# Attention and channel MLP in one stream: the last down weights, the first stores, the row copies and the start of the projection moved

## The chip, the core and the metric

The kernel runs on one core of a Trainium2 chip. The core has five engines with an instruction queue each: TensorE (PE; matmuls, with weight loads shown apart as PEld), VectorE (DVE), ScalarE (ACT), GpSimd (POOL) and SyncE (SP), which here only issues DMAs. An engine takes its instructions in the order in which the program writes them, so an instruction that waits holds everything behind it on that engine. DMAs are issued from an engine's queue and run beside the engines; instructions wait for their landing. Matmuls read the core's on-chip memory and write banks of PSUM, of which the kernel keeps small pools.

The metric is the device time of one execution in microseconds. Several runs are made and their median is taken.

## What is computed

The input `x` has 2048 tokens of 576 numbers. The result mixes two branches by a gate of each token:

```python
g = sigmoid((x * gate_w).sum(-1, keepdims=True))
a = softmax(q k^T * 18**-0.5) v  @ wo      # 32 heads of 18, q, k, v = x @ wqkv
b = gelu(layernorm(x) @ w1 + b1) @ w2 + b2 # 576 -> 4608 -> 576, tanh form of gelu
out = g * a + (1 - g) * b
```

All of it is float32 in and out. The kernel multiplies in a faster, rounded form of float32: most operands are split into a rounded high part and a low part (what the rounding left over), and a product is the sum of three matmuls (high by high, low by high, high by low).

## The kernel before

**First stage (up to about 255 us).** `x` is loaded in four blocks of 512 tokens, transposed, split and multiplied by `wqkv`. The parts of q and k go to a DRAM buffer `qk_scr`, v to `v_scr` (one store of a token tile behind each second `v_group`, L788), the normalised tokens of the MLP to `y_scr`. In the last block the generator of the MLP is started between the groups; its third step, called as `between()` inside the last `v_group`, loads the low parts of the first y block (`load_y(0, 1, ...)`, six DMAs).

**The loop (512 steps).** Sixteen pairs of heads times two halves of the queries make 32 units `u` of 16 steps `kc`. A step has two half steps. Each computes two banks of scores (`s2`, L247), takes their exponentials on ScalarE (L250) and does a round of the row maxima for the next unit (`s1_round`: matmul L206, maximum on VectorE L208). Every second step multiplies two blocks of probabilities by v (`pv`, L265). When a unit's maxima are all there, `s1_finish` turns them into two rows (high and low part) per head and `rows()` transposes them (L223), copies them to the tile `mr` (L225) and writes them with four DMAs (through `dma_r`, L121) into rows 54, 55, 118 and 119 of the unit's query tile `QA[u % 3]`, so that the score matmul subtracts the maximum by itself. In the loop this happens at step 12 of the unit before. At a unit's end `o_store` copies the sums out (L277) and sends them to DRAM (L279, L285); 12 slots later `spread` takes the reciprocals of the denominators on VectorE (L288) and stores them (L289), and 16 slots after that `wide` writes them out for every row (L297).

**Slots.** `run_due` counts slots: one behind every `s2`, every `pv` and every fill, seven in two steps. `defer(n, fn)` writes `fn` into the program n slots later. `bg` is a list of work for GpSimd, written out when the kernel's own estimate of GpSimd's queue (`pool_end - now`) is below a bound: 950 ns for an up block, 3800 ns for a down block, and its raw data counts as landed (`LOADED`; in the loop 8 slots after the load for an up block). This is all decided when the program is written out, not on the chip.

**The MLP inside the loop.** Three times in two steps `fill` writes a piece of the MLP between the attention's matmuls (`atom`). The MLP has four blocks of 512 tokens (`tb`, their y tiles loaded by `load_y`, L121 `big<-y_scr`) and nine groups `g` in each, 36 groups `i`, two pairs `q` of 128-wide chunks in a group. `h_pair` does the up matmuls of a pair (L443); the gelu of it runs on VectorE, ScalarE (L464, L496, L494) and mostly GpSimd (L162), which ends with a high and a low part `hh`, `hl` of each chunk. `outs` does the down matmuls of a group in four output pairs, one for each tile of 128 tokens (`out_pair`, L523, summed on VectorE L532). In the last group of a block the second pair is put inside `outs` of the group before, ahead of its output pair `t == 2` (`inner`): its `hh` and `hl` are kept in a tile of the up weights' pool.

In the first block the weights are raw: `load_w1` (L346) and `load_w2` (L352) load them into one `x` tile, `split` rounds the high part on ScalarE (L367), takes the low part on GpSimd (L162), and stores both to `w1_scr` and `w2_scr` (L372). In the other blocks they are reloaded from there (L121 `w<-w_scr`). Up weights have three places (`wp1`), down weights four (`wp2`), which is one group: `prep_w2(i)` loads the four tiles of group i once `outs(i - 1)` has been written, and each load waits until its place is read for the last time. When a block is done, its result is scaled by the gate on GpSimd (L536) and stored to `b_scr` (L539).

**The projection.** At steps 489, 494, 497 and 499 (`PSTEP`) the generator `out_proj` is called: it loads `wo` (L890, split on GpSimd L883 and L884), the first block of attention sums (`load_o`), their reciprocals (`load_den`), and plans their product (`normed`: L957 and L967 on VectorE, L960 on ScalarE). Once the MLP is over, its last store has been written (`kept == NT`) and step 500 is past, `fill` writes pieces of the projection (L1030): 14 matmuls for half a row tile, then L1034 on VectorE adds `b` from the tile that `load_b` loaded (L945). What is left follows the loop.

## Time and profile before

| | us |
|---|---|
| median of 3 runs | 2382.97 |
| lowest, highest run | 2378.87, 2385.91 |
| the profiled execution | 2379.91 |
| its span, first to last instruction | 2378.1 |

| engine | busy us | share of the span |
|---|---|---|
| TensorE | 2308.8 | 97% |
| VectorE | 1655.4 | 70% |
| ScalarE | 1425.9 | 60% |
| GpSimd | 968.3 | 41% |

Times within the trace count from the span's start. A row of the timeline gives start, length, engine, line, operation, what it writes and reads (by the program's own names, `out<-in`), the number of instructions merged into it, and in brackets how long the engine had been idle before it and what ended that. "SPq" is SyncE's queue: the length of such a row is the time for which it was issuing, not that of the transfer. The granted clock is the share of TensorE's full clock that it was given in a stretch.

### The profile page before, as it was taken

What the parts mean: (1) busy time and instruction counts of PE and PEld (TensorE: products, weight loads), DVE (VectorE), ACT (ScalarE), POOL (GpSimd) and SP (SyncE); (2) the same over time, 40 slices, a digit from 0 to 9 for tenths busy, and PEclk for the clock granted to TensorE, in tenths of its full rate; (3) what the DMA queues carried; (4) which work ended last, traced back from release to release, by engine and by line L of the source; (5) the groups of instructions that cost most, each with busy time, mean ns of one, the idle gap of its engine ahead of it and who ended that gap; (6) DMA issues with size and microseconds to landing.
All of it is one profiled execution on the core that took longest, in us unless ns stands there. A gap on an engine that the chain in (4) does not pass through costs nothing.

```text
span 2378.1 us, 51603 instructions
## 1 busy us (share of the span) xinstructions
PE 2308.8 (97%) x20585; PEld 1571.9 (66%) x20585; DVE 1655.4 (70%) x2890; ACT 1425.9 (60%) x2628; POOL 968.3 (41%) x964
## 2 busy tenths in 40 slices
PE   8999899999999999999999999999999999999889
PEld 7876566666666666666666666666656666666558
DVE  5467577777776777777777777777767777777424
ACT  4222367777676666666666666666656666666552
POOL 3001366666664433333454444433343334444500
PEclk9999899999999999999999999999999999999899
DMA  7748744545455423342354424232545343331254
GB/s 229 243 166 235 211 146 137 166 129 151 134 185 163 156 94 116 104 140 97 98 153 161 130 85 131 94 116 94 142 137 166 112 119 114 92 115 66 96 181 157
DMA packets 164874, 330.31 MB, mean 139 GB/s; under 512 B 57898, under 2 KB 84558, under 8 KB 153906
## 3 DMA queue, kind: packets, MB, share of 16 engines
q1 hardware_dynamic: 163050, 323.78, 43.4%
q8 instruction: 162, 2.65, 0.5%
q10 hardware_dynamic: 1584, 3.24, 0.4%
q14 instruction: 78, 0.64, 0.1%
HBM read 234.16 MB, written 96.58 MB: 139 GB/s over the span
## 4 chain that ended last, share of the span: by engine, by line
PE 89%; DMA 5%; DVE 3%; SPq 1%; issue 1%; ACT 0%; POOL 0%; DVEq 0%; ACTq 0%
PE ps L523 20%; PE ps L265 19%; PE ps L443 18%; PE ps L247 12%; PE ps L206 11%; PE ps L755 4%; PE ps L1030 2%; PE ps L776 2%; DVE m L208 1%; DMA big<-y_scr 1%; DMA x<-in_B_w_dram 1%; DMA v_scr<-vt 0%; PE ps L682 0%; SPq L121 0%; SPq L372 0%
## 5 line engine op out<-in xcount | busy, mean ns | idle before, releaser
L208 DVE TENSOR_REDUCE m<-ps 128x1 f32<-128x512 f32 x2048 | 1316.7, 685 | 478.5 <-PE ps L206 460.1
L250 ACT ACTIVATE p<-ps 128x512 f32<-128x512 f32 x1368 | 742.9, 596 | 435.9 <-PE ps L247 425.6
L162 POOL TENSOR_SCALAR zz<-zz 128x512 f32<-128x512 f32 x288 | 179.4, 623 | 843.6 <-ACT zz L496 828.6
L443 PE MATMUL ps<-big,w 64*128 64x512 f32 x3888 | 513.9, 394 | 0.1
L523 PE MATMUL ps<-w,hh 64*128 64x288 f32 x4352 | 491.2, 300 | 19.3 <-DMA w<-w_scr 7.1
L250 ACT ACTIVATE ring<-ps 128x512 f32<-128x512 f32 x680 | 369.4, 596 | 213.3 <-PE ps L247 206.5
L206 PE MATMUL ps<-ka,qa 54*128 54x512 f32 x2048 | 457.0, 416 | 14.3 <-DVE m L208 7.9
L247 PE MATMUL ps<-qa,ka 56*128 56x512 f32 x2048 | 455.3, 425 | 10.9 <-ACT p L250 5.3
L523 PEld LDWEIGHTS ps<-w,hh 64*128 64x128 f32 x4352 | 383.6, 186 | 76.2 <-issue 45.2
L443 PEld LDWEIGHTS ps<-big,w 64*128 64x128 f32 x3888 | 380.1, 186 | 76.9 <-ACT z L464 0.4
L162 POOL TENSOR_TENSOR zz<-zz,z 128x512 f32<-128x512 f32 x288 | 372.5, 1294 | 24.0
L247 PEld LDWEIGHTS ps<-qa,ka 56*128 56x128 f32 x2048 | 205.5, 185 | 227.8 <-DVE m L208 176.6
L265 PE MATMUL ps<-p,vt 128*32 128x512 f32 x2736 | 348.7, 604 | 2.7 <-DMA vt<-v_scr 2.7
L523 PE MATMUL ps<-w,hl 64*128 64x288 f32 x2176 | 334.6, 292 | 0.0
L206 PEld LDWEIGHTS ps<-ka,qa 54*128 54x128 f32 x2048 | 213.5, 187 | 87.8 <-ACT p L250 24.1
L162 POOL TENSOR_TENSOR w<-x,w 128x576 fp32r<-128x576 f32 (+1 forms) x54 | 98.5, 1837 | 317.2 <-DMA y_scr<-hh 169.1
L523 PEld LDWEIGHTS ps<-w,hl 64*128 64x128 f32 x2176 | 218.5, 185 | 4.9
L162 POOL TENSOR_TENSOR hl<-zz,hh 128x512 fp32r<-128x512 f32 x136 | 176.6, 1299 | 11.3
L265 PE MATMUL ps<-ring,vt 128*32 128x512 f32 x1360 | 180.5, 603 | 0.0
L265 PEld LDWEIGHTS ps<-p,vt 128*32 128x32 f32 x2736 | 72.0, 109 | 164.1 <-issue 153.7
L532 DVE SCALAR_TENSOR_TENSOR x<-ps,x 128x288 f32<-128x288 f32 x256 | 104.1, 449 | 23.7 <-PE ps L523 23.7
L755 PE MATMUL ps<-big,wqk 128*128 128x512 f32 x432 | 111.7, 408 | 2.9 <-ACT wqk L676 2.3
(98 smaller groups left out, 1374.4 us busy)
## 6 DMA issues: line engine op xcount, KB each, us to landing
w<-w_scr SPq DMA_DIRECT2D x54, 1152.0 KB
w<-w_scr SPq DMA_DIRECT2D x108, 576.0 KB
x<-in_B_w_dram SPq DMA_DIRECT2D x72, 288.0 KB
w_scr<-w SPq DMA_DIRECT2D x18, 1152.0 KB
w_scr<-w SPq DMA_DIRECT2D x36, 576.0 KB
big<-y_scr SPq DMA_DIRECT2D x42, 384.0 KB
qa<-qk_scr SPq DMA_DIRECT2D x192, 72.0 KB
ka<-qk_scr SPq DMA_DIRECT2D x84, 144.0 KB
```

The source lines that it names most:

```text
L162: fn(*args, **kw)
L206: nc.tensor.matmul(ps, qa[r0:r0 + 54, t * P:(t + 1) * P], ka[r0:r0 + 54, kb * TB:(kb + 1) * TB], start=True, stop=True)
L208: nc.vector.tensor_reduce(M4[u][:, h, t, kb:kb + 1], ps, axis=AX.X, op=ALU.max)
L247: nc.tensor.matmul(ps[h], ka[r0:r0 + 56, kc * P:(kc + 1) * P], qa[r0:r0 + 56, qb * TB:(qb + 1) * TB], start=True, stop=True)
L250: nc.scalar.activation(RING[n % 3][:, qb, h], ps[h], AF.Exp, scale=SCALE)
L265: nc.tensor.matmul(OB[u][r:r + 32, :], v[:, k, 19 * h:19 * h + 32], RING[c % 3][:, qb, h, :], start=(k == 0), stop=(k == NT - 1))
L443: nc.tensor.matmul(ps[h], wt[w_][r, c, :], Y[s_][r, c, :], start=(k == 0), stop=(k == 26))
L523: nc.tensor.matmul(ps[nn][:, :ND], h_[r, tok], w_[p_][r, cs[nn]], start=(k == 0), stop=(k == 6 * G - 1))
L532: nc.vector.scalar_tensor_tensor(dst, ps[nn][:, :ND], 0.5, b2b[:, cs[nn]] if g == 0 else dst, op0=ALU.mult, op1=ALU.add)
L755: nc.tensor.matmul(ps, w_[:, c, ms], big[:, s_, :], start=(k == 0), stop=False)
L776: nc.tensor.matmul(ps[:, :ND], big[:, s_, tok], w_[:, c, cs], start=(k == 0), stop=False)
L1030: nc.tensor.matmul(ps[:, :ND], OT[b][2][:, s_, tok], w_part(w_, c)[:, cs], start=(k == 0), stop=(k == 13))
```

## The change

Eight edits:

1. `rows()` writes its rows with two DMAs instead of four, and issues them from ScalarE's queue instead of SyncE's when fewer than `BUSY` = 20 slots have passed since the last `load_y`.
2. `spread` is deferred by 20 slots instead of 12 (but for the last two units).
3. Before the loop, the store of a split down block is deferred by 44 slots instead of 20, and the load that follows the third up block by 6 slots instead of 16.
4. The four down tiles of the last group go into two places of the up weights' pool (`borrow_w2`): the first two behind that group's first pair, the other two one slot after its second pair; `prep_w2` is not called for it.
5. In the last block the inner pair stands ahead of the output pair `t == 1` instead of `t == 2`.
6. The last `v_group` stores v ahead of `between()` instead of behind it.
7. `load_b_first` loads the first two row tiles of `b` at step 497, into `QA[0]` and `VT[0]`; `load_b(0)` loads the other two.
8. `fill` looks at its start, not at its end, whether the projection can begin.

```diff
@@ -40,6 +40,7 @@
 SLOT = 950.0
 LAND = 8
 GAP = 1130.0
+BUSY = 20
 TOTAL = NB * NG * (G // 2 * 27 * 231 + 8 * 3 * G * 131)
 PLAN = [[(), (0,), (1,), (2,), (3,), (4,), (5, 6), ()], [(), (), (0,), (1,), (2,), (3,), (4,), (5, 6)],
         [(0,), (1,), (2,), (3,), (4,), (5,), (6,), ()]]
@@ -122,6 +123,7 @@
 
 
     slot = [0]
+    inflow = [-BUSY]
     later = []
 
     def defer(n, fn):
@@ -224,11 +226,10 @@
             mr = asm.tile([32, P], F32R, name="mr", bufs=1)
             nc.scalar.activation(mr, ps[:32, :P], AF.Copy)
             qa = QA[u % 3]
+            queue = nc.scalar if looped[0] and slot[0] - inflow[0] < BUSY else nc.sync
             for h in range(2):
-                for b in range(2):
-                    r = 64 * h + 54 + b
-                    k = (h * 2 + b) * 8
-                    dma_r(nc.sync, qa[r:r + 1, :].rearrange("o (t n) -> o t n", n=P), mr[k:k + 8, :].bitcast(F32))
+                r = 64 * h + 54
+                dma_r(queue, qa[r:r + 2, :].rearrange("b (t n) -> b t n", n=P), mr[16 * h:16 * h + 16, :].bitcast(F32))
         if looped[0]:
             ROWS.append(rows)
         else:
@@ -297,7 +298,7 @@
             nc.sync.dma_start(dst.rearrange("(h d) n -> h d n", d=DH), dn_scr[u][:, None, :].to_broadcast([2, DH, HALF]))
             stored.append(u)
         if u < NU - 1:
-            defer(12 if u < NU - 2 else 4, spread)
+            defer(20 if u < NU - 2 else 4, spread)
         else:
             spread()
 
@@ -369,8 +370,8 @@
 
             def second(t):
                 pool_op(src.free_size(), nc.gpsimd.tensor_tensor, t[:, 1], src, t[:, 0].bitcast(F32), op=ALU.subtract)
-                defer(4 if looped[0] else 20, lambda: nc.sync.dma_start(scr, t.bitcast(F32)))
-                defer(3 if looped[0] else 1 if raw != (1, 2) else 16, lambda: then(raw[1]))
+                defer(4 if looped[0] else 20 if raw[0] == 1 else 44, lambda: nc.sync.dma_start(scr, t.bitcast(F32)))
+                defer(3 if looped[0] else 1 if raw != (1, 2) else 6, lambda: then(raw[1]))
                 table[key] = (t[:, 0], t[:, 1])
 
             queue = raw[0] ** 2 * SLOT
@@ -409,6 +410,14 @@
                         continue
                     split(W2, (q, j), wp2, [P, 2, D], (2, c), R2[c % 2], w2_scr[c],
                           lambda c: load_w2(c + 2))
+
+        def borrow_w2(q):
+
+            t = wp1.tile([P, 2, 9, P], F32R, name="w4").rearrange("p a b c -> p (a b c)")
+            for j in range(2):
+                part = t[:, 2 * j * D:2 * (j + 1) * D].rearrange("p (a d) -> p a d", d=D)
+                dma_r(nc.sync, part, w2_scr[2 * (q % NQ0) + j])
+                W2[q, j] = (part[:, 0], part[:, 1])
 
         open_pairs = [0]
 
@@ -543,6 +552,7 @@
             yield 131
 
         def load_y(tb, s_, c0=0, c1=9):
+            inflow[0] = slot[0]
             if s_ not in Y:
                 Y[s_] = big_tile()
             for h in range(2):
@@ -554,7 +564,7 @@
             if g == 0:
                 ACC[tb] = x_tile().rearrange("p (t d) -> p t d", t=4)[:, :, :D]
             for t in range(4):
-                if t == 2:
+                if t == (1 if tb == NB - 1 else 2):
                     yield from between
                 yield from out_pair(i, t, ACC[tb])
             for j in range(G):
@@ -579,6 +589,8 @@
             i, m, _ = chunk(q)
             if m == 1 and seq[i][1] == NG - 1:
                 hidden[0] = seq[i][0]
+                if i == n - 1:
+                    defer(1, lambda: borrow_w2(q))
 
 
 
@@ -589,9 +601,11 @@
             if i < n:
                 yield from pair(q, held, last=i > 0)
                 prep(q + 1 + held)
+                if i == n - 1:
+                    borrow_w2(q)
             if i > 0:
                 yield from outs(i - 1, pair(q + 1, 2, inner=True) if inside else ())
-            if 0 < i < n:
+            if 0 < i < n - 1:
                 prep_w2(i)
             if i < n and not inside:
                 yield from pair(q + 1, held)
@@ -783,9 +797,9 @@
                 nc.scalar.activation(dst, src, AF.Copy)
             else:
                 nc.vector.tensor_copy(dst, src)
+                nc.sync.dma_start(v_scr[4 * tb + t], VT[t % 2])
                 if between is not None:
                     between()
-                nc.sync.dma_start(v_scr[4 * tb + t], VT[t % 2])
 
         load_x(0)
         load_w(0)
@@ -941,8 +955,15 @@
             ready.add(b)
 
         def load_b(b):
-            BT[b] = io.tile([P, 4, D], F32, name="bt", bufs=2)
-            nc.sync.dma_start(BT[b], b_scr[b * TB:(b + 1) * TB, :].rearrange("(t p) d -> p t d", p=P))
+            t0 = len(BT.setdefault(b, []))
+            bt = io.tile([P, 4 - t0, D], F32, name="bt", bufs=2)
+            nc.sync.dma_start(bt, b_scr[b * TB + t0 * P:(b + 1) * TB, :].rearrange("(t p) d -> p t d", p=P))
+            BT[b] += [bt[:, t] for t in range(4 - t0)]
+
+        def load_b_first():
+            BT[0] = [QA[0].bitcast(F32)[:, :D], VT[0].rearrange("p k e -> p (k e)")[:, :D]]
+            for t, dst in enumerate(BT[0]):
+                nc.sync.dma_start(dst, b_scr[t * P:(t + 1) * P, :])
 
         tmp = {}
 
@@ -995,6 +1016,7 @@
         load_o(0)
         yield 0
         load_den(0)
+        load_b_first()
         yield 0
         for c in range(7):
             defer(c, lambda c=c: normed(0, c))
@@ -1031,7 +1053,7 @@
                             k += 1
                             if k < 14:
                                 yield 122.5
-                    nc.vector.scalar_tensor_tensor(res[:, cs], ps[:, :ND], gate[:, tt:tt + 1], BT[b][:, t, cs],
+                    nc.vector.scalar_tensor_tensor(res[:, cs], ps[:, :ND], gate[:, tt:tt + 1], BT[b][t][:, cs],
                                                    op0=ALU.mult, op1=ALU.add)
                     if b + 1 < NB:
                         waiting.extend((b + 1, stage) for stage in PLAN[b][2 * t + n])
@@ -1054,16 +1076,16 @@
 
     def fill(step, share):
 
+        if over[0] is None and not stream and kept[0] == NT and step > PSTEP[-1] + 1:
+            stream.append(proj)
+            over[0] = step
+            spent[0] = 0.0
         if over[0] is None:
             piece[0] = share
             behind[0] = base + (TOTAL - base) * step / FIN
             t = spent[0]
             atom()
             run_due(max(spent[0] - t, GAP))
-            if not stream and kept[0] == NT and step > PSTEP[-1] + 1:
-                stream.append(proj)
-                over[0] = step
-                spent[0] = 0.0
         else:
             filler(spent[0] + FILL)
             run_due()
```

## The prediction, made before the changed kernel ran

> **What bounds the kernel now.** I read the page first, its engine table, the clock row and the chain of waits:
>
> ```profile
> span 2378.1 us, 51603 instructions
> PE 2308.8 (97%) x20585; PEld 1571.9 (66%) x20585; DVE 1655.4 (70%) x2890; ACT 1425.9 (60%) x2628; POOL 968.3 (41%) x964
> PE 89%; DMA 5%; DVE 3%; SPq 1%; issue 1%; ACT 0%; POOL 0%; DVEq 0%; ACTq 0%
> ```
>
> TensorE is busy 97% of the span and holds 89% of the chain. The change removes no matmul, so it can only win where PE stands idle, 69.3 us in all (2378.1 - 2308.8), and where PE runs at half clock behind an idle stretch. Next I read PE's timeline for its longest waits; the bracket is the idle time ahead of the instruction and what ended it:
>
> ```profile
> 268.75 1.92 PE L265 MATMUL ps<-p,vt 128*32 128x512 f32 x16 [2.66 <-DMA vt<-v_scr]
> 296.54 0.79 PE L247 MATMUL ps<-qa,ka 56*128 56x512 f32 x1 [5.26 <-ACT p L250]
> 740.56 0.49 PE L206 MATMUL ps<-ka,qa 54*128 54x512 f32 x1 [1.40 <-DVE m L208]
> 1740.35 1.17 PE L247 MATMUL ps<-qa,ka 56*128 56x512 f32 x2 [4.23 <-DMA qa<-mr]
> 2245.16 0.85 PE L523 MATMUL ps<-w,hh 64*128 64x288 f32 x4 [6.82 <-DMA w<-w_scr]
> 2249.87 0.61 PE L523 MATMUL ps<-w,w 64*128 64x288 f32 x2 [2.27 <-DMA w<-w_scr]
> 2279.96 0.49 PE L247 MATMUL ps<-qa,ka 56*128 56x512 f32 x1 [1.26 <-ACT ring L250]
> 2295.25 2.29 PE L1030 MATMUL ps<-big 128*128 128x288 f32 x8 [5.23 <-DVE res L1034]
> ```
>
> These eight are 29.1 us. Last, the table by stretches of 5 us right behind them (after the length: busy time of PE, PEld, DVE, ACT, POOL; then granted clock, DMA share, GB/s):
>
> ```profile
> 295.00:300.00 5.00, 3.46 (x15) 2.70 (x17) 1.29 (x2) 3.47 (x6) 3.84 (x3) 0.50 0.25 107
> 300.00:305.00 5.00, 5.00 (x38) 2.71 (x38) 3.24 (x5) 3.71 (x7) 4.66 (x6) 0.87 1.02 299
> 740.00:745.00 5.00, 4.44 (x23) 1.52 (x25) 3.02 (x6) 0.31 (x2) 0.00 (x0) 0.66 0.25 82
> 1740.00:1745.00 5.00, 4.65 (x20) 1.37 (x20) 1.29 (x2) 1.09 (x2) 0.00 (x0) 0.50 0.02 5
> 2245.00:2250.00 5.00, 2.31 (x14) 1.68 (x14) 0.00 (x0) 0.00 (x0) 0.51 (x1) 0.50 1.02 405
> 2250.00:2255.00 5.00, 4.92 (x42) 4.28 (x42) 0.01 (x1) 2.17 (x4) 0.00 (x0) 0.63 0.51 149
> 2280.00:2285.00 5.00, 5.00 (x24) 2.60 (x28) 0.59 (x1) 3.40 (x7) 0.06 (x1) 0.66 0.79 271
> 2295.00:2300.00 5.00, 4.75 (x22) 2.73 (x26) 1.22 (x3) 1.09 (x2) 0.00 (x0) 0.50 1.06 383
> 2300.00:2305.00 5.00, 5.00 (x33) 2.77 (x26) 1.11 (x2) 2.54 (x5) 0.00 (x0) 0.85 0.82 282
> ```
>
> Half of the busy time spent at clock 0.50 is lost (a mean of 0.66 over 5 us is 3.4 us at half). That adds 1.7 + 0.65 = 2.4 us behind the stall at 291, 1.7 at 739, 2.3 at 1736, 1.15 + 1.85 = 3.0 at 2238, 1.7 at 2279, 2.4 + 0.75 = 3.1 at 2290. [...]
>
> **Part by part, the start.** The queue and ScalarE rows (SPq is SyncE's queue; its length is issue time):
>
> ```profile
> 249.48 3.92 SPq L121 DMA_DIRECT2D big<-y_scr  x6
> 253.50 0.53 SPq L788 DMA_DIRECT2D v_scr<-vt  x1
> 265.05 0.38 SPq L192 DMA_DIRECT2D vt<-v_scr  x1
> 275.91 9.11 SPq L372 DMA_DIRECT2D w_scr<-w  x4
> 285.12 2.61 SPq L346 DMA_DIRECT2D x<-in_B_w_dram  x2
> 294.84 1.16 ACT L367 ACTIVATE w<-x 128x1152 fp32r<-128x1152 f32 x1 [6.51 <-issue]
> ```
>
> *V store ahead of `between`.* The last v store now goes 0.53 us ahead of the six y loads instead of 3.92 behind them. The V load, which waits for it to land and stood at the head of the queue until 265.05, follows right behind the y loads, near 254.5, and shares the engines with nothing but them. Gain 0 to 2.66; I take 2.2, because the V store pushes the y loads back a little and the third piece of the first pair reads the last of them.
>
> *Raw weights ahead of stores.* ScalarE's rounding of the fourth raw up block was next in its queue at 288.3 (294.84 - 6.51) and stood there, the exponentials behind it, because its load was issued at 285.12, behind four weight stores that took 9.11 us to issue. The load's slot goes from 54 to 44, ahead of all four, and the down stores among them go to slots 67 to 72: it is issued near 275.9. Does the copy move forward with it? By the kernel's bookkeeping no. The load counts as landed at slot 52 instead of 62, but the copy also waits until GpSimd's planned queue is under 950 ns; worked by hand that queue is 1155 ns at slot 52, never under 950 until slot 64, and 21 at slot 65, where the copy stands before and after. So the data comes 9.2 us sooner (near 285.6) and the copy's turn 2.2 sooner (286.1): just in time. Gain 5.26 + 2.4 = 7.7; I take 7.2. Lower end 0: the moved stores (three of one size, one of twice that, 9.11 us) stand ahead of the next raw load and make the same 6.5 us wait there. I lean away from it because that copy's turn, by the same bookkeeping, comes near slot 79.
>
> **The block changes.**
>
> ```profile
> 739.71 0.25 DVE L288 RECIPROCAL dn<-dn 128x16 f32<-128x16 f32 x1 [2.77 <-DMA ot_scr<-oe]
> 1217.47 2.72 SPq L121 DMA_DIRECT2D qa<-mr  x4
> 1715.55 10.59 SPq L121 DMA_DIRECT2D big<-y_scr  x12
> 1723.57 0.25 ACT L225 ACTIVATE mr<-ps 32x128 fp32r<-32x128 f32 x1
> 1727.37 6.55 SPq L121 DMA_DIRECT2D qa<-mr  x4
> ```
>
> *Reciprocals later.* At 736.9 VectorE began to wait for sums whose DMA stood behind the y loads; the maxima behind it held PE 1.40 us. Two steps hold seven slots and last 6.5 us (from 2261.50 to 2268.02 in the rows below), so eight more slots are 7.4 us: the reciprocal comes near 744.3, after the landing at 739.7. Gain 1.4 to 1.4 + 1.7; I take 3.1. The work stays 0.25 us per unit. The broadcast store behind it is also 8 slots later, 36 after the unit's end; the step that needs it in the projection comes 59 slots after unit 29's end.
>
> *Rows on ScalarE's queue.* The rows of unit 23 were ready at 1723.8, issued behind twelve y loads from 1727.37 to 1733.9 and landed at 1740.35. Only this unit falls within 20 slots behind y loads. At the other changes the rows come ahead of them (at 1217.47 with the y loads next in the queue), and they merely go from four DMAs to two, as everywhere else. ScalarE now issues two DMAs in its own queue, 6.55 / 4 = 1.64 us each at most (that price is the backlog of the y loads). The rows then have 12 us until PE asks at 1736.1. Upper gain 4.23 + 2.3 = 6.5; lower -3.3 (3.3 us of held exponentials and nothing won). I take 5.9: ScalarE is idle 40% of the span and covers most of two issues, whose price without a backlog is 2.72 / 4 = 0.68. [...]
>
> **The end.**
>
> ```profile
> 2226.75 0.67 POOL L883 TENSOR_SCALAR big<-x 128x576 fp32r<-128x576 f32 x1
> 2241.13 1.88 SPq L121 DMA_DIRECT2D w<-w_scr  x4
> 2244.25 1.26 POOL L162 TENSOR_TENSOR w<-zz,w 128x512 fp32r<-128x512 f32 x1
> 2261.50 0.82 DVE L532 SCALAR_TENSOR_TENSOR x<-ps,x 128x288 f32<-128x288 f32 x2 [5.69 <-PE ps L523]
> 2268.02 0.82 DVE L532 SCALAR_TENSOR_TENSOR x<-ps,x 128x288 f32<-128x288 f32 x2 [1.34 <-PE ps L523]
> 2279.47 1.12 DVE L969 TENSOR_TENSOR big<-x,hh 64x512 fp32r<-64x512 f32 x1
> 2294.68 0.94 DVE L1034 SCALAR_TENSOR_TENSOR res<-ps,gate,bt 128x288 f32<-128x288 f32 x2 [14.08 <-DMA bt<-b_scr]
> ```
>
> *Borrowed places and the sooner pair.* The last group waited twice over at 2238.3: for its four down tiles, issued at 2241.13 once the group before had released them, and for its second pair's activations, which GpSimd finished at 2245.5 because the five splits of `wo` (from 2226.75, 10.7 us) had slipped in ahead. Both edits are needed. The first borrowed place is that of a pair finished a whole group earlier; the second is free when the inner pair ends, three output pairs of 6.5 us (2261.50 to 2268.02) ahead of use, against the 8.7 us that the four loads took from issue to the last landing. With the pair one output pair earlier, its GpSimd work is written ahead of the splits and ends near 2245.5 - 10.7 - 6.5 = 2228. Gain 6.82 + 2.27 + 3.0 = 12.1; lower end 3.0, if GpSimd still ends at 2245.5.
>
> *Projection one fill sooner.* Its first nine matmuls move into the ScalarE-bound gap ending at 2279.96. Normalising its first block ends at 2280.6 (2279.47 + 1.12), so they may wait in turn. Gain 0 to 1.26 + 1.7 = 3.0; I take 1.5.
>
> *First two b tiles early.* The first result stood 14.08 us for its b tile. Two of the four row tiles now load into places free since step 496, ahead of the next block's loads. What is late next is that block's denominators, which VectorE takes right behind the second result: they are ahead of the b loads in the same queue, so landed by 2294.7 at the latest, some 2 us after VectorE would reach the third result. Gain 5.23 + 3.1 = 8.3, lower end 8.3 - 2 - 1.7 = 4.6; I take 7.5.
>
> Sum: 2.2 + 7.2 + 3.1 + 5.9 + 12.1 + 1.5 + 7.5 = **39.5 us**. The profiled execution took 2379.91 us (span 2378.1 and 1.8 around it), so it would take 2340.4. The median of the runs, 2382.97, stands 3.1 above it: 2343.5.
>
> **The rivals.** *The start's wait comes back* at the next raw load, or the load still lands late: 7.2 lost and 2.2 with it, 2353. For it, the margin of half a microsecond; against, the copy's fixed slot. *The rows gain nothing*: their packets start only when the y packets end, as on SyncE's queue (landing at 1740.35), 2343.5 + 5.9 = 2349. For it: the rows landed only when the twelve loads were through. Against it: they stood 3.5 us unissued, and every packet of the y loads was ahead of them in one queue, which they now leave. [...] *GpSimd stays late in the last group*: 12.1 becomes 3.0, 2352.6; for it the splits' place, against it that they are not registered before step 489. *The end is not PE's*: if the last unit's chain set the finish, 12.1 + 1.5 + 7.5 would vanish, 2364.6; the rows 2250 to 2305 with PE at 4.75 to 5.00 speak against it. *Slower*: SyncE waits in order for each reciprocal, and the weight reloads behind it wait too:
>
> ```profile
> SPq L289 <- DVE dn L288: 64.7, 13, 7.6
> PE ps L523 <- DMA w<-w_scr: 9.3, 3, 6.8
> ```
>
> Holds reach 7.6 us now, yet no reload outside the last group made PE wait (its 9.3 us are those above). If 8 slots more pushed reloads past their cover in each of 30 units, the kernel would be slower from 39.5 / 30 = 1.3 us a unit; 2 us a unit give 2404.
>
> **How the numbers follow.** Forecast 2343.5 with 0.60; start 0.13; rows 0.08; GpSimd 0.10; end not PE's 0.03; slower 0.03; nothing beyond the noise, parts cancelling, 0.03. About 0.3% (7.1 us) is what a measurement of this kernel tells from no change. The first five cases lie beyond it: faster 0.94, same 0.03, slower 0.03. All upper ends add up to 43.4; from the fastest run, 2378.87, that is 2335.5, and I put the low end at 2334. The high end, 2366, holds two of the lesser cases together (9.4 + 9.1 on 2343.5 is 2362) and the end not being PE's.
>
> **What would show it.** Right: no ScalarE wait at the fourth raw copy and V landed before the first PV; no reciprocal waiting at the first block change; rows issued by ScalarE near 1711 and landed before PE asks; PE without idle between the last two groups, GpSimd's last activations ahead of the `wo` splits; the first result without a wait; granted clock near 1.00 in all these places. Wrong: a new idle stretch of PE over 2 us in the first 60 us of the loop, exponentials held behind ScalarE's DMA issue, or an unchanged finish in spite of gaps closed.

## The result and the profile after

| | before | after |
|---|---|---|
| median of the runs, us | 2384.44 (2378.87 to 2387.66, 4 runs) | 2341.06 (2340.19 to 2341.99, 4 runs) |
| span of the profiled execution, us | 2378.1 | 2339.5 |
| TensorE busy, us | 2308.8 | 2297.5 |
| mean granted clock of TensorE | 0.987 | 0.994 |

The ratio of the times is 0.9816, with a 95% interval of 0.9803 to 0.983: some 43 us less by the medians, 38.6 us by the two spans. The page of the kernel after has the same busy work on the other engines; on the chain of waits, PE's share rose from 89 to 94% and DMA's fell from 5 to 1%:

```profile
PE 2297.5 (98%) x20585; PEld 1571.1 (67%) x20585; DVE 1655.2 (71%) x2890; ACT 1424.9 (61%) x2628; POOL 966.3 (41%) x964
PE 94%; DVE 3%; issue 1%; DMA 1%; ACT 1%; SPq 0%; ACTq 0%; DVEq 0%
```

The lines of the code have slightly higher numbers now: the scores L248, the maxima L208 and L210, the value product L266, the raw rounding L368, the row copy L227, the reciprocal L289, the projection L1052 with L1056. To see where the time came from I take the start of the k-th value product in both traces and subtract: the difference moves only where one kernel gains on the other.

**The start.** SyncE's queue and ScalarE's copy of the fourth raw block, then TensorE at the first value product:

```profile
252.16 0.33 SPq L800 DMA_DIRECT2D v_scr<-vt  x1
252.59 3.92 SPq L122 DMA_DIRECT2D big<-y_scr  x6
256.61 0.55 SPq L194 DMA_DIRECT2D vt<-v_scr  x1
...
273.98 6.64 SPq L347 DMA_DIRECT2D x<-in_B_w_dram  x2
280.66 4.14 SPq L373 DMA_DIRECT2D w_scr<-w  x4
```

```profile
288.47 1.17 ACT L368 ACTIVATE w<-x 128x1152 fp32r<-128x1152 f32 x1
```

```profile
269.00 1.92 PE L266 MATMUL ps<-p,vt 128*32 128x512 f32 x16 [1.22 <-DMA vt<-v_scr]
```

The V load is issued 8.4 us sooner than before (256.61 against 265.05), the raw load at 273.98 ahead of four weight stores, and the copy has no bracket: it waited for nothing. The wait at the first value product fell only from 2.66 to 1.22 us. The DMA view of the stretch from 264 to 269 us says why:

```profile
DMA packets 2241, 1.44 MB, mean 287 GB/s; under 512 B 2080, under 2 KB 2080, under 8 KB 2147
```

The V load's packets are 208 B each, 2048 of them, and almost all packets of that size stand in this stretch; from 257 to 264 only 64 packets are under 512 B. So the V load, though issued 8.4 us sooner, moved only when the six y loads ahead of it in the same queue were through: from 264.5 on, where it had moved from 266.1 on in the kernel before. The difference grows to 7.7 us by the fourth pair of steps, although the first stage itself was 1.7 us slower in this execution.

**The block changes.** VectorE meets its reciprocal without a wait (735.20 below; in the kernel before it had stood there for 2.77 us). At the third change the rows go out on ScalarE's queue:

```profile
735.20 0.24 DVE L289 RECIPROCAL dn<-dn 128x16 f32<-128x16 f32 x1
```

```profile
1702.60 19.15 SPq L122 DMA_DIRECT2D big<-y_scr  x12
```

```profile
1710.89 1.91 ACTq L122 DMA_DIRECT2D qa<-mr  x2
1712.85 1.08 ACT L251 ACTIVATE p<-ps 128x512 f32<-128x512 f32 x2 [1.98 <-PE ps L248]
```

```profile
1713.49 0.99 PE L208 MATMUL ps<-ka,qa 54*128 54x512 f32 x2 [1.07 <-ACT p L251]
```

```profile
1715.00:1720.00 5.00, 4.92 (x42) 3.94 (x44) 2.50 (x6) 2.67 (x6) 4.24 (x5) 0.66 0.70 145
```

ScalarE is taken for 1.91 us by the two issues. The exponentials behind them start at 1712.85 (the bracket names the scores, but these had ended by 1710.9; the 1.98 us are the two issues, which do not count as busy), TensorE stands 1.07 us for them and then has a clock of 0.66 over 5 us, that is 3.4 us at half and 1.7 us lost. The 4.23 us wait for the rows is gone. By the value products this place gave 3.5 us, not 5.9.

The y loads' row is 19.15 us long where it was 10.59, and the table of waits (waiting engine and line, what ended it, us in all, times, longest) says why: eight of the twelve were issued by 1709.5, and the ninth, at 1719.17, had waited 9.7 us for the rows to land. Below it, the packets on ScalarE's queue (q10) between 1717.4 and 1718.7: all 36 that it moved at this block change. The table by stretches has the DMA share (last but one) falling from 1.00 at that moment:

```profile
SPq L122 <- DMA qa<-mr: 9.7, 1, 9.7
```

```profile
q10 hardware_dynamic: 36, 0.02, 8.1%
```

```profile
1718.00:1719.00 1.00, 1.00 (x12) 1.00 (x12) 0.25 (x1) 0.14 (x1) 0.92 (x2) 0.52 0.35 70
1719.00:1720.00 1.00, 1.00 (x14) 0.33 (x14) 0.89 (x3) 0.65 (x2) 1.00 (x2) 1.00 0.00 0
```

So the rows, issued by 1712.8, landed only when the engines had worked off the eight loads, near 1719. They had eight loads ahead of them instead of twelve, and they passed none of the eight. No data join a y load to these rows; that it waits for them is what the trace says. The trace's records name the same completion semaphore (109) for the ninth load and for the first of the two row DMAs, which would explain the wait; no run tested it.

**The end.** GpSimd now ends the last pair before the first split of `wo` begins, the borrowed places are loaded from 2176.88 on, and the first result finds its `b` tile (its operand is `qa`, the borrowed tile; 0.76 us is TensorE's product, not the load):

```profile
2209.49 1.29 POOL L164 TENSOR_TENSOR w<-zz,w 128x512 fp32r<-128x512 f32 x1
2210.75 0.68 POOL L897 TENSOR_SCALAR big<-x 128x576 fp32r<-128x576 f32 x1
```

```profile
2176.88 0.82 SPq L122 DMA_DIRECT2D w<-w_scr  x2
```

```profile
2225.00:2230.00 5.00, 5.00 (x56) 2.99 (x53) 0.82 (x2) 3.33 (x8) 0.75 (x1) 1.00 0.87 304
```

```profile
2251.72 0.52 DVE L1056 SCALAR_TENSOR_TENSOR res<-ps,gate,qa 128x288 f32<-128x288 f32 x1 [0.76 <-PE ps L1052]
...
2263.58 0.69 DVE L978 TENSOR_TENSOR x<-x,den 128x512 f32<-128x512 f32 x1 [5.94 <-DMA den<-ot_scr]
```

TensorE runs at full clock through the last group. What is late next is VectorE at the denominators (2263.58, 5.94 us), with one wait of TensorE behind it:

```profile
2265.52 0.50 PE L248 MATMUL ps<-qa,ka 56*128 56x512 f32 x1 [1.02 <-ACT p L251]
```

### The profile page after: what moved, and what is told of

The parts are those of the page before. It is cut to its first block, busy times and chain, and to the rows that moved or that the text cites. A ratio compares the mean times of both kernels' runs of the same rounds, so it can differ in the third digit from the quotient of the medians.

```text
span 2339.5 us, 51512 instructions
## 1 busy us (share of the span) xinstructions
PE 2297.5 (98%) x20585; PEld 1571.1 (67%) x20585; DVE 1655.2 (71%) x2890; ACT 1424.9 (61%) x2628; POOL 966.3 (41%) x964
## 4 chain that ended last, share of the span: by engine, by line
PE 94%; DVE 3%; issue 1%; DMA 1%; ACT 1%; SPq 0%; ACTq 0%; DVEq 0%
PE ps L532 21%; PE ps L266 20%; PE ps L452 19%; PE ps L248 13%; PE ps L208 11%; PE ps L769 4%; PE ps L1052 3%; PE ps L790 2%; DVE m L210 1%; PE ps L696 1%; DMA vt<-v_scr 1%; DVE p L756 0%; PE ps L772 0%; PE ps L771 0%; DMA p<-in_A_wqkv_dram 0%
## 5 line engine op out<-in xcount | busy, mean ns | idle before, releaser
L210 DVE TENSOR_REDUCE m<-ps 128x1 f32<-128x512 f32 x2048 | 1316.5, 685 | 465.0 <-PE ps L208 448.1
L208 PE MATMUL ps<-ka,qa 54*128 54x512 f32 x2048 | 456.0, 415 | 12.1 <-DVE m L210 5.0
L248 PE MATMUL ps<-qa,ka 56*128 56x512 f32 x2048 | 453.8, 423 | 1.2 <-ACT p L251 1.0
L248 PEld LDWEIGHTS ps<-qa,ka 56*128 56x128 f32 x2048 | 205.2, 184 | 214.8 <-DVE m L210 178.8
L266 PE MATMUL ps<-p,vt 128*32 128x512 f32 x2736 | 344.8, 598 | 1.2 <-DMA vt<-v_scr 1.2
L208 PEld LDWEIGHTS ps<-ka,qa 54*128 54x128 f32 x2048 | 213.7, 187 | 84.4 <-ACT p L251 25.3
L266 PEld LDWEIGHTS ps<-p,vt 128*32 128x32 f32 x2736 | 71.6, 109 | 160.8 <-issue 151.8
L266 PE MATMUL ps<-ring,vt 128*32 128x512 f32 x1360 | 179.1, 598 | 0.0
L541 DVE SCALAR_TENSOR_TENSOR x<-ps,x 128x288 f32<-128x288 f32 x256 | 104.1, 448 | 12.7 <-PE ps L532 12.7
```

What stands on the lines that cost most here:

```text
L208: nc.tensor.matmul(ps, qa[r0:r0 + 54, t * P:(t + 1) * P], ka[r0:r0 + 54, kb * TB:(kb + 1) * TB], start=True, stop=True)
L210: nc.vector.tensor_reduce(M4[u][:, h, t, kb:kb + 1], ps, axis=AX.X, op=ALU.max)
L248: nc.tensor.matmul(ps[h], ka[r0:r0 + 56, kc * P:(kc + 1) * P], qa[r0:r0 + 56, qb * TB:(qb + 1) * TB], start=True, stop=True)
L266: nc.tensor.matmul(OB[u][r:r + 32, :], v[:, k, 19 * h:19 * h + 32], RING[c % 3][:, qb, h, :], start=(k == 0), stop=(k == NT - 1))
L541: nc.vector.scalar_tensor_tensor(dst, ps[nn][:, :ND], 0.5, b2b[:, cs[nn]] if g == 0 else dst, op0=ALU.mult, op1=ALU.add)
```

## The experiments

Each edit is against the kernel after. All twelve, with the median of their runs, the ratio to the kernel before and the span of the trace less 2339.5:

| run | median, us | ratio (95% interval) | span |
|---|---|---|---|
| e1 rows on SyncE's queue | 2343.30 | 0.9815 (0.9801 to 0.983) | +1.9 |
| e2 no borrowed places | 2354.06 | 0.9864 (0.9848 to 0.9881) | +13.4 |
| e3 pair one output pair later | 2349.04 | 0.9846 (0.9831 to 0.9861) | +8.1 |
| e4 no early `b` tiles | 2350.61 | 0.985 (0.9836 to 0.9865) | +7.9 |
| e5 start's order as before | 2346.01 | 0.9843 (0.9823 to 0.9863) | +4.1 |
| e6 reciprocals as before | 2346.34 | 0.9847 (0.9826 to 0.9867) | +3.6 |
| e7 rows ahead of the last y loads | 2338.77 | 0.9809 (0.9789 to 0.9829) | -2.3 |
| e8 the same, plan later | 2337.56 | 0.9805 (0.9785 to 0.9825) | -2.5 |
| e9 V store behind y loads | 2342.89 | 0.9825 (0.9811 to 0.984) | +2.5 |
| e10 only the raw load's slot undone | 2340.93 | 0.9815 (0.9801 to 0.983) | +0.4 |
| e11 rows on GpSimd's queue | 2339.81 | 0.981 (0.9795 to 0.9825) | -1.5 |
| e12 projection one fill later | 2342.53 | 0.9823 (0.9809 to 0.9836) | +1.6 |

The intervals are some 6 to 10 us wide, so an effect under 4 us is read from the traces. There the first stage, in which nothing was changed but the V store, differs by itself: the first value product starts between 266.88 and 271.32 us. Effects below are therefore counted from it on, by the value products.

**e1: rows on SyncE's queue.**

```diff
-            queue = nc.scalar if looped[0] and slot[0] - inflow[0] < BUSY else nc.sync
+            queue = nc.sync
```

> The changed kernel with the rows of every unit issued on SyncE's queue again (still two DMAs of two heads). My theory: only the unit at the third block change notices. TensorE's wait near 1736 comes back (about 4.2 us, ended by the DMA of the rows, and some 2 us at half clock behind it), while the wait of 1.07 us near 1712, for exponentials that stood behind ScalarE's two DMA issues, and the half clock behind that one go. Net +3 to +4 us, near 2344.5. Rival one (a second issuing engine saves nothing but issue time): time unchanged, 2341, with the rows landing as soon as in the changed kernel. Rival two (the rows were worth the 5.9 us of my sum and the ScalarE wait has another cause): +5.9, 2347, with the wait near 1712 still there.

SyncE's queue, then TensorE:

```profile
1700.70 10.67 SPq L122 DMA_DIRECT2D big<-y_scr  x12
1712.63 3.06 SPq L122 DMA_DIRECT2D qa<-mr  x2
```

```profile
1725.33 1.28 PE L248 MATMUL ps<-qa,ka 56*128 56x512 f32 x2 [4.07 <-DMA qa<-mr]
```

```profile
1724.00:1726.00 2.00, 0.67 (x3) 0.47 (x4) 0.00 (x0) 0.00 (x0) 0.00 (x0) 0.55 0.16 30
```

The wait for the rows is back (1721 to 1725; the 1736 of the expectation is the place of before), and the wait of 1.07 us at the exponentials is gone. Counted from the first value product the kernel loses 4.0 us (1.87 + 2.13), as expected. The median of the runs, 2.2 us up, can't show that by itself. The rows, behind all twelve loads, landed when the DMA engines had run dry (a share of 1.04 from 1722 to 1724, then 0.16). Both rivals fall as to the time; whether a second queue passes the first is not shown by it.

**e11: the same rows on GpSimd's queue.**

```diff
-            queue = nc.scalar if looped[0] and slot[0] - inflow[0] < BUSY else nc.sync
+            queue = nc.gpsimd if looped[0] and slot[0] - inflow[0] < BUSY else nc.sync
```

> The changed kernel with the rows of a unit that ends soon behind y loads issued on GpSimd's queue instead of ScalarE's. My theory: the gain comes from leaving SyncE's queue and the loss from holding the exponentials, so on GpSimd, which has no exponentials, the rows land in time without the wait of 1.07 us near 1712: -1.5 to -2.8 us, 2338.5 to 2339.5. Rival (GpSimd's own work at the block change, 3.8 us of 5 busy, is on the path, and two issues there cost what they cost on ScalarE or more): 0 to +3 us, with TensorE waiting for GpSimd or for the rows.

GpSimd's issue, and the stretch in which the next unit's scores ask for the rows (at 1725.19):

```profile
1712.74 1.34 POOL L122 DMA_DIRECT2D qa<-mr  x2 [14.04 <-ACT mr L227]
```

```profile
1724.00:1726.00 2.00, 2.00 (x28) 1.54 (x28) 1.80 (x4) 1.40 (x3) 1.83 (x3) 1.00 1.06 228
```

TensorE doesn't wait, ScalarE isn't held, and the kernel gains 2.7 us by the block change, from 1.44 behind to 1.23 ahead. GpSimd's issue cost TensorE nothing; GpSimd had just been waiting for 14 us. The DMA view gives 8.0 us from issue to landing for these two. By stretches it gives each queue's packets, MB and share of the engines' time; first GpSimd's queue (q0) from 1718.9 to 1720.4, then SyncE's (q1) from 1720.4 to 1727.5:

```profile
q0 software_dynamic: 64, 0.02, 10.2%
```

```profile
q1 hardware_dynamic: 716, 1.34, 87.4%
```

All packets of GpSimd's queue moved in the first of these stretches, and SyncE's queue still had 1.34 MB to move behind them, over three loads of 384 KB. Only one of the twelve loads was issued later than the first of the rows (at 1713.55), so here the rows passed more than two loads that had been issued ahead of them. Measured from the first y load (1704.16, in e1 1700.70) the rows were issued 8.6 us later here and 11.9 in e1, and landed within some 16 us against 24.6. Issuing sooner is 3.3 us of these 8, and passing loads the rest. The time needed only the first part: counted by packets, the eleventh load was through at 1724.8, so rows behind eleven loads would still have come just ahead of 1725.19.

**e7: rows on SyncE's queue, with a third of the y loads held back.**

```diff
-            queue = nc.scalar if looped[0] and slot[0] - inflow[0] < BUSY else nc.sync
+            queue = nc.sync
...
-                    load_y(tb + 1, 0, loaded, (k + 1) // 3)
-                    load_y(tb + 1, 1, loaded, (k + 1) // 3)
+                    def fetch(c0=loaded, c1=(k + 1) // 3):
+                        load_y(tb + 1, 0, c0, c1)
+                        load_y(tb + 1, 1, c0, c1)
+                    if k == 26:
+                        defer(8, fetch)
+                    else:
+                        fetch()
```

> The changed kernel with all rows on SyncE's queue, and the last piece of a block's y loads held back eight slots so that the last unit's rows are issued ahead of it. My theory: the backlog of the y loads is what makes both ways dear. Without ScalarE's DMA issues the wait of 1.07 us near 1712 and 3.4 us at half clock behind it (1.7 us lost) go, and the rows have landed before TensorE asks: -2 to -3 us, 2338.5. Rival (the rows' packets still stand behind the earlier y loads' packets): TensorE waits for the rows near 1736 again, +3, 2344.

```profile
1704.36 5.33 SPq L122 DMA_DIRECT2D big<-y_scr  x8
1712.65 1.40 SPq L122 DMA_DIRECT2D qa<-mr  x2
1714.14 4.66 SPq L122 DMA_DIRECT2D big<-y_scr  x4
```

The two issues take 1.40 us on an engine that has nothing else to do, the rows stand behind eight loads instead of twelve, as they came to do in the kernel after, and no wait is left at the block change. From 1.36 behind at the first value product the kernel is 1.66 ahead after the change: 3.0 us. A further 1.0 us came at 2264, where TensorE's wait of 1.02 us is no longer there. By their medians this kernel and e8 are the fastest that ran: all runs of e7 (2337.27 to 2338.97) lie under all of the kernel after, but the intervals of the ratios, each against its own runs of the kernel before, overlap.

**e8: e7 and the projection's plan.**

```diff
-PLAN = [[(), (0,), (1,), (2,), (3,), (4,), (5, 6), ()], [(), (),
+PLAN = [[(), (), (0,), (1,), (2,), (3,), (4,), (5, 6)], [(), (),
```

> The same as the kernel with the rows ahead of the last y loads, and the first half of the projection's plan of normalising put one result later. My theory: VectorE's wait of 5.9 us for denominators near 2258 then comes behind the next result instead of ahead of it, and TensorE's idle time of 1.0 us near 2264 and what it has of clock loss go: a further -1 us, 2337.5. Rival: the normalised blocks are then late for the next matmuls and TensorE waits there instead: 0 to +2 against the kernel without this plan.

VectorE at the denominators:

```profile
2262.83 0.69 DVE L984 TENSOR_TENSOR x<-x,den 128x512 f32<-128x512 f32 x1 [3.75 <-ACT p L251]
```

The wait moved behind the next result, as meant (the bracket names ScalarE's exponentials now and not the denominators' DMA, so what ended it is open), but the TensorE wait that this was to remove had already gone in e7. The spans are 0.2 us apart and the runs overlap (2336.24 to 2338.83): whether the plan does anything is not shown.

**e2 and e3: the two halves of the last group's edit.**

```diff
-            if 0 < i < n - 1:
+            if 0 < i < n:
                 prep_w2(i)
...
-                if t == (1 if tb == NB - 1 else 2):
+                if t == 2:
```

e2 has the first hunk and no call of `borrow_w2`, e3 the second alone.

> The changed kernel with the last group's down weights reloaded into their own places as before, and the last inner pair kept one output pair earlier. My theory: both edits were needed, so the four loads end the wait of the last group's first output pair again: some 6 to 9 us of idle TensorE plus 2 to 3 us of clock, 2350 to 2352.5. Rival (GpSimd's lateness was the only bound, the loads were hidden behind it): +0 to 2 us, 2341 to 2343.

> The changed kernel with the last inner pair back at the third output pair of the group before, the borrowed places kept. My theory: the last group's second half waits for GpSimd, which has the splits of the output weights ahead of the pair's parts and ends near 2243: TensorE idles 4 to 7 us and loses 2 us of clock, +6 to 9 us, 2347 to 2350. Rival (the loads were the only bound): +0 to 1 us.

TensorE in e2, then GpSimd and TensorE in e3:

```profile
2229.15 0.85 PE L532 MATMUL ps<-w,hh 64*128 64x288 f32 x4 [5.60 <-DMA w<-w_scr]
```

```profile
2220.80 0.62 POOL L164 TENSOR_SCALAR zz<-zz 128x512 f32<-128x512 f32 x1
```

```profile
2227.55 0.72 PE L532 MATMUL ps<-w,w 64*128 64x288 f32 x4 [2.24 <-POOL w L164]
```

Without the borrowed places the loads end TensorE's wait, and the whole costs 11.5 us (13.4 - 1.9). With the pair late, GpSimd comes out of the last split at 2220.8 and TensorE follows it tile by tile; cost 8.3 us. Together 19.8 us, more than the 12.7 that both edits won: two causes lay over each other, and each alone would have left most of the stall. Both rivals (one cause only) fall.

**e4: no early `b` tiles.**

```diff
         load_den(0)
-        load_b_first()
```

> The changed kernel without the two early b loads: every b tile is loaded when its turn comes. My theory: the first result waits for its b tile again, TensorE idles about 5 us near 2255 with some 3 us of half clock behind it: +7.4 us, 2348.5, the term 7.5 of my sum. Rival (VectorE would wait for the next block's denominators near 2264 in any case and this wait absorbs most of it): +1 to 3 us, 2342 to 2344.

VectorE and TensorE:

```profile
2263.20 0.94 DVE L1055 SCALAR_TENSOR_TENSOR res<-ps,gate,bt 128x288 f32<-128x288 f32 x2 [14.03 <-DMA bt<-b_scr]
```

```profile
2263.78 2.29 PE L1051 MATMUL ps<-big 128*128 128x288 f32 x8 [8.48 <-DVE res L1055]
```

VectorE waits 14.03 us, as in the kernel before (14.08), but TensorE's share is 8.48 us instead of 5.23. The projection starts a fill sooner: its first matmul (2246.72, before 2280.38) stands 16.5 us ahead of the end of VectorE's wait, where it stood 14.3 us ahead, which accounts for 2.2 of the 3.3 us. The edit is worth 9.4 us here, from 1.65 ahead of the kernel after to 7.7 behind it. The rival with the denominators falls.

**e5 and e10: the numbers of the start.**

```diff
-                defer(4 if looped[0] else 20 if raw[0] == 1 else 44, lambda: nc.sync.dma_start(scr, t.bitcast(F32)))
-                defer(3 if looped[0] else 1 if raw != (1, 2) else 6, lambda: then(raw[1]))
+                defer(4 if looped[0] else 20, lambda: nc.sync.dma_start(scr, t.bitcast(F32)))
+                defer(3 if looped[0] else 1 if raw != (1, 2) else 16, lambda: then(raw[1]))
```

e5 undoes both, e10 the second alone.

> The changed kernel with the two numbers of the start undone: the weight stores of all raw blocks wait 20 slots and the first raw load 16 slots, as before; the V store stays ahead. My theory: ScalarE's fourth raw copy waits again for its load behind four weight stores, TensorE idles about 5 us near 290 and runs at half clock for 4 to 5 us behind it: +7.5 us, 2348.5. The two idle times of 0.8 us near 444 and 633 of the kernel before may come back with it (another 2 us), as the other raw blocks' stores and copies take their old slots. Rival (the wait has only moved to a later raw load): 0, 2341.

> The changed kernel with the first raw load 16 slots behind its mark again, the stores of the later raw blocks still 44 slots behind theirs. My theory: the load's turn (slot 54) now comes behind the stores of the first blocks only, not behind all four, so it is issued 4 to 5 us sooner than with both numbers undone: ScalarE's copy waits under 2 us and TensorE idles under 1 us: +0 to 1.5 us, 2341.5. Rival (the load's own slot carries the whole gain and moving the stores does nothing): the wait of 3.4 us and a spell of half clock as with both numbers undone, +5.8 us in the progress of the first 300 us.

SyncE's queue and ScalarE in e5, and the same two rows in e10:

```profile
276.51 7.86 SPq L373 DMA_DIRECT2D w_scr<-w  x4
284.47 2.64 SPq L347 DMA_DIRECT2D x<-in_B_w_dram  x2
```

```profile
294.47 1.16 ACT L368 ACTIVATE w<-x 128x1152 fp32r<-128x1152 f32 x1 [4.68 <-DMA x<-in_B_w_dram]
```

```profile
279.90 2.10 SPq L347 DMA_DIRECT2D x<-in_B_w_dram  x2
```

```profile
288.35 1.17 ACT L368 ACTIVATE w<-x 128x1152 fp32r<-128x1152 f32 x1 [0.50 <-DMA x<-in_B_w_dram]
```

With both undone the copy waits 4.68 us and the value products lose 5.8 us (from 1.2 to 7.0) by the fourth pair of steps; the wait has not moved elsewhere, and the expected 7.5 was too much because the copy came to its turn later than in the kernel before. With the load's slot alone undone, the copy waits 0.50 us and the loss is 0.6 us: the moved stores alone carry all but that of the 5.8 us. Whether the load's slot alone would do as much was not run. The two idle times near 444 and 633 did not come back in e5 (there is one of 0.45 us at 641). By the end 2.9 of the 5.8 us are left (4.1 - 1.2): the half clock at the third block change and TensorE's wait at 2264, 1.5 us each in the progress, are not there in e5.

**e6: reciprocals 12 slots behind.**

```diff
-            defer(20 if u < NU - 2 else 4, spread)
+            defer(12 if u < NU - 2 else 4, spread)
```

> The changed kernel with the reciprocals 12 slots behind a unit's end again. My theory: only the first block change notices: VectorE waits some 2.8 us for the sums near 730, TensorE 1.4 us for the maxima behind it, and 3.4 us at half clock: +3.1 to 3.3 us, 2344.3. Rival one: other idle stretches have moved so that the reciprocal no longer meets the y loads: 0. Rival two: the two idle times of 0.8 us near 444 and 633 in the kernel before were also VectorE's at a reciprocal: then they come back too and it costs 5 us, 2346.

VectorE, then TensorE:

```profile
733.01 0.25 DVE L289 RECIPROCAL dn<-dn 128x16 f32<-128x16 f32 x1 [3.78 <-DMA dn<-oe]
```

```profile
437.36 0.50 PE L208 MATMUL ps<-ka,qa 54*128 54x512 f32 x1 [0.81 <-DVE m L210]
...
625.86 0.50 PE L208 MATMUL ps<-ka,qa 54*128 54x512 f32 x1 [0.81 <-DVE m L210]
...
733.86 0.49 PE L208 MATMUL ps<-ka,qa 54*128 54x512 f32 x1 [2.40 <-DVE m L210]
```

Besides the known wait, two more of 0.81 us come back, at the places where the kernel before had 0.80 and 0.82 us: the second rival holds as to the time, and the edit is worth 5.6 us by step 118 (from 0.2 ahead to 5.4 behind), not 3.1; 3.8 are left at the end, for the same two reasons as in e5. That the deferral brings these two is shown; how is not, and the rival's reason (VectorE standing at a reciprocal) does not fit: the unit's reciprocal starts at 406.2 us, 30 us earlier, without a wait of TensorE.

**e9: V store behind the y loads.**

```diff
-                nc.sync.dma_start(v_scr[4 * tb + t], VT[t % 2])
                 if between is not None:
                     between()
+                nc.sync.dma_start(v_scr[4 * tb + t], VT[t % 2])
```

> The changed kernel with the last V store issued behind the six y loads again. My theory: the V load starts some 4 us later; the first value product waits 2.4 to 2.7 us instead of 1.0 to 1.4, and as the raw load now stands ahead of the stores, nothing else is late: +1.2 to 1.5 us, 2342.4. Rival (the first value product is held by the first stage and the copies as well, so that the V load's place does not matter): 0, with the same wait of 1.0 to 1.4 us.

TensorE, and the stretch behind it:

```profile
271.19 3.60 PE L266 MATMUL ps<-p,vt 128*32 128x512 f32 x16 [3.64 <-DMA vt<-v_scr]
```

```profile
270.00:275.00 5.00, 3.81 (x18) 0.88 (x20) 0.00 (x0) 0.00 (x0) 3.15 (x3) 0.66 0.88 319
```

The wait is 2.4 us longer than with the store ahead (3.64 - 1.22), and 1.7 us of clock go behind it, which did not happen behind the 2.66 us wait of the kernel before (clock 1.00 in the same stretch). So the theory is right in kind and low in size; the rival falls.

**e12: projection one fill later**, with the start of the projection at the end of `fill` as before.

```diff
-        if over[0] is None and not stream and kept[0] == NT and step > PSTEP[-1] + 1:
-            stream.append(proj)
...
             run_due(max(spent[0] - t, GAP))
+            if not stream and kept[0] == NT and step > PSTEP[-1] + 1:
+                stream.append(proj)
```

> The changed kernel with the projection's matmuls registered at the end of the step as before, one fill later. My theory: TensorE idles again for 1.2 to 1.3 us ahead of a score product near 2240, with 0 or 1.7 us of clock loss by chance behind it: +1.2 to 3 us, 2342.3 to 2344. Rival (the nine matmuls wait for the normalised block either way and the gain is not theirs): 0 to +0.5 us.

```profile
2250.75 0.49 PE L248 MATMUL ps<-qa,ka 56*128 56x512 f32 x1 [1.26 <-ACT ring L251]
```

The wait of 1.26 us is back (at 2249, not 2240) and costs 1.6 us by the value product at 2262, but the one after it is only 0.4 us late: TensorE's later wait of 1.02 us at 2264.5 isn't there. By the last value product 0.1 us is left. Behind it, where only the projection remains, the projection's matmuls alone (busy time of PE and PEld, clock, DMA share, GB/s), in e12 and in the kernel after:

```profile
2292.80:2341.10 48.30, 41.20 (x305) 40.48 (x304) 0.99 0.42 145
```

```profile
2292.36:2339.50 47.14, 40.01 (x296) 39.29 (x295) 1.00 0.39 136
```

Nine matmuls more are left for the end in e12, and the end is 1.2 us longer. From the first value product to the end the edit is worth 1.3 us (1.6 - 0.3), the lower end of what the theory gave, but by the matmuls left for the end more than by the wait that it named. The rival (0 to 0.5 us) falls.

## Why the prediction was right, step by step

Forecast 2343.5, measured 2341.06; the sum of 39.5 us stands against 38.6 in the spans. The gains by the value products, counted in the two traces:

| step | predicted | before against after | undone alone |
|---|---|---|---|
| V store ahead | 2.2 | 1.4 (the wait) | 4.1 (e9) |
| raw weights ahead of stores | 7.2 | 8.0 | 5.8 (e5) |
| reciprocals later | 3.1 | 3.3, and 1.9 at two other places | 5.6 (e6) |
| rows on ScalarE's queue | 5.9 | 3.5 | 4.0 (e1) |
| borrowed places and sooner pair | 12.1 | 12.7 | 11.5 (e2), 8.3 (e3) |
| projection one fill sooner | 1.5 | 1.2, and 0.6 behind the last value product | 1.3 (e12) |
| first two `b` tiles | 7.5 | 7.4 | 9.4 (e4) |

The eight long waits and the half clock behind them were the right account: closing them gave nearly what they held. But for the rows' term, the terms agree with the traces within a microsecond, the reciprocals' at their own place; the column at the right differs from them where edits share a stall (e2, e3, e4) or a clock spell fell otherwise (e9). The V store won 1.4 of the 2.2 us forecast, and its sign of being right, V landed before the first value product, did not come: the six y loads held the V load up for longer than the prediction allowed.

**The mis-sized term is the rows'.** The prediction said that ScalarE "is idle 40% of the span and covers most of two issues, whose price without a backlog is 2.72 / 4 = 0.68". The two issues took 1.91 us, 0.96 each, between SyncE's price without backlog (0.68) and the 1.64 with it. More important, the 40% idle is a mean: in this stretch the next scores wait for ScalarE's exponentials, so 1.91 us there became 1.07 us of idle TensorE and 1.7 us lost at half clock. The upper gain of 6.5 less these 2.8 is 3.7, close to the 3.5 counted. Exponentials held behind ScalarE's issue were on the prediction's own list of what would show it wrong.

**The reason given for that step holds in part.** The prediction argued that the rows "stood 3.5 us unissued, and every packet of the y loads was ahead of them in one queue, which they now leave". The first half held: issuing sooner is 3.3 us between e1 and e11. The second is not seen in the kernel after, where the rows on ScalarE's queue landed with the last of the eight loads ahead of them; it is seen in e11, where the rows on GpSimd's queue passed more than two loads. That need not be a difference of the two queues: counted by packets, some four loads moved between the issue of the rows and the rows themselves in both traces, and in the kernel after no further load stood ahead that they could have passed. In the kernel after, the two DMAs of 8 KB took 7 to 8 us from issue to landing; in e11 they landed some 8 us sooner than in e1, counted from the first y load, and only 3.3 us of that are issue time. In the kernel after, an issue 3.6 us sooner (8.3 us behind the first y load, 11.9 in e1) and four loads fewer ahead were enough. e7 gets the same from SyncE's queue alone, by order.

**What the sum left out.** The two idle times of 0.8 us near 444 and 633 were not among its rows. Their 1.9 us replaced most of the 2.4 that the rows lacked, and the raw weights won 0.8 more than forecast, as much as the V store lacked; that the total is closer than its terms is luck.

**The rivals.** The start's wait did not come back: the copy at 288.47 has no bracket, and in e10 a raw load issued 5.9 us later (279.90) made the copy wait only 0.50 us, so the margin was wider than the half microsecond feared. GpSimd did not stay late: it ended the pair at 2210.78 and the splits followed. The end was TensorE's: 21.3 us of the predicted 21.1 (12.7 + 1.2 + 7.4 against 12.1 + 1.5 + 7.5) reached the finish. The later reciprocals made no weight reload late: SyncE stood for a reciprocal up to 15.3 us at a time (7.6 before), yet no wait of TensorE in the loop is ended by a weight load any more.

## What to carry to other kernels

Here a small DMA behind large ones was helped by what stood ahead of it when it was issued: behind eight y loads instead of twelve the rows cost TensorE no wait in e7, against 4.07 us in e1. So put it in front by order. Another engine's queue issued it sooner (3.6 us on ScalarE's, 3.3 on GpSimd's, counted from the first y load; in e11 it also came past loads issued before it), and that engine's work in that very stretch, not its share of the span, said what the issue cost: 1.07 us of idle TensorE behind ScalarE, none behind GpSimd. Where one stall has two causes, undo each alone: both here cost most of the stall by themselves (11.5 and 8.3 us, where both edits together won 12.7). Add the half clock behind a stall to its price, but as a range, since the same stall has it in one trace and not in another (1.7 us lost in the kernel after, none in e4).

## What the runs showed of the chip

**The price of the same idle time differs from trace to trace.** A wait of 1.07 to 1.09 us behind ScalarE's issues stands in the traces of the kernel after, e3, e4, e5 and e6. In two (after, e3) the clock is 0.66 over 1715 to 1720 us, that is 3.4 us at half; in three (e4, e5, e6) it stays at 1.00 in all stretches up to 1725 us. The rows of the kernel after are above; the stretch of e4, behind the same wait (1.09 us, ending at 1713.36):

```profile
1715.00:1720.00 5.00, 4.92 (x51) 3.01 (x52) 3.40 (x7) 2.98 (x6) 4.37 (x5) 1.00 0.81 163
```

In the traces of the kernels before and after, every spell of half clock in the loop lasts 3.41 us or two or four times that. Before: 6.83 us from 294.48, 3.41 from 741.63, 6.83 from 1738.32, 13.65 from 2240.08, 3.41 from 2281.04 and 6.83 from 2294.70. After: 3.41 from 1715.55 alone; the idle time of 1.27 us among its projection's matmuls near 2297 has none behind it (clock 1.00 from 2290 to 2339). From each of the six starts before to the next it is 447.15, 996.69, 501.76, 40.96 and 13.66 us: 131, 292, 147, 12 and 4 times 3.413 to 3.415. What decides whether a spell follows an idle time was not shown.

**One edit shifts a later wait.** TensorE's wait of about 1 us at 2264 in the kernel after is gone, or down to 0.2 us, in e5, e6, e7 and e11, which touch nothing near it, and in e12: VectorE waited for the same denominators for 3.8 to 5.1 us there (2.4 in e12) instead of 5.94. Up to a microsecond of any single edit's price is therefore not its own, nor are the 1.7 us lost at half clock behind ScalarE's issues, which come in some traces and not in others.
